# A sparse-attention and MLP kernel: first batch by casting loads, band of v gated, AV in four PSUM banks, w_out in 8 KB runs

## The chip, the cores and the metric

The kernel runs on one core of one Trainium2 chip. The core has five engines that run side by side: TensorE (PE; its weight loads are listed apart as PEld), VectorE (DVE), ScalarE (ACT), GpSimd (POOL) and SyncE (SP). Each works through its own list of instructions in order, and semaphores join the lists. Sixteen DMA engines move data between the chip's memory (HBM) and the core's SBUF. DMAs are issued by SP and ACT (the queues q1 and q10 of the profile) or by POOL (q0); only those of POOL convert float32 to float16 on the way. The metric is the time of one execution on the device in microseconds (us).

## The reference

Eight batches, eight heads, 576 positions, 64 values a head. Heads 0 to 3 attend to the last 32 positions (local heads), heads 4 to 7 to all earlier positions that agree modulo 32 (strided heads). The result is the input of a two-layer MLP.

```
mask_local   = (rel >= 0) & (rel < 32)
mask_strided = (rel >= 0) & (pos[None] % 32 == pos[:, None] % 32)
scores = np.where(masks, q @ k.T / 8, -1e9)
attn = softmax(scores);  x = (attn @ v) as 4608 tokens x 512
h = x @ w_in                    # 512 x 2048
g = s * relu(h) ** 2 + b
out = g @ w_out                 # 2048 x 512, float32
```

## The kernel before

**Tiles.** A batch's heads are worked in four pairs: 0 and 1 local, 2 and 3 strided. A pair is a chain: transpose q and k on PE (`trans`, L328), copy them out of PSUM (L271, on ACT or DVE), scores (L383), exp on ACT (L396), mask on DVE (L404), the product with v (AV, L432), whose last column is the sum of the weights, reciprocal (L446) and multiplication (L450) on DVE into `x_nat`, transpose back (L471), copy into `xT` (L271). One AV group of six or four matmuls uses one PSUM bank, and there is one such bank (tag `a`, `AB = 1`), so the next group waits for the multiplication of the group before it.

**MLP.** The tokens are cut into nine blocks of 512. FF1 (L507) is 64 matmuls a block, in groups of four over `xT[0..3]`, ReLU on ACT (L522), square on DVE (L526). FF2 (L541) is 64 matmuls a block, evicted by DVE (L552) and stored by SP. `bcs` (L564) is the constant row that b adds, 16 matmuls with w_out, needed before the first FF2 eviction.

**Loads.** For batch 0, q, k and v come as float32 by SP and ACT into staging areas (two 16 KB tiles of the pool `gT`, and `w_out_sb`, not yet in use), and are cast to float16 by ACT and DVE (`pair_post`, `cast_s`, `cast_v`). The v of the local heads is the band: for each block of 96 queries the 128 keys that it sees, 256 bytes a run, five DMAs (L210, L212). The v of batch 1 goes the same way. POOL copies one element of the staged k into `gate` (L617), which holds back everything behind it on POOL: w_in (four DMAs), q and k of batch 1, w_out (four DMAs, after the casts have read the staging area in `w_out_sb`), then q, k and v of batches 2 to 7 by casting loads.

**Order of the work.** The class `Plan` sets the order of every engine's list when the kernel is built. It keeps a clock of its own, takes costs and landing times from constants (`landing`, `plan.done`), and at each step emits a PE step that is ready by that clock; copies and casts go to ACT or DVE, whichever would be done first. The order is then fixed. If a landing comes later than assumed, the engine waits at that instruction, with all that stands behind it.

Of the kernel before, what the change touches and what calls it, by code (L numbers as in the profile page):

```python
# [106 lines left out]
def kernel(  # L107
# [31 lines left out]
    for p in range(SQ):  # L139
        for c in range(SQ):  # L140
# [39 lines left out]

    stage0 = gp.tile([128, 4096], FP32, tag="gT", name="stage0")
    stage1 = gp.tile([128, 4096], FP32, tag="gT", name="stage1")
    stage2 = w_out_sb.rearrange("p f m -> p (f m)").bitcast(FP32)
    NL, NS = 4 * LT * D, 4 * ST * D
    st_q = {"ql": stage0[0:LQ, 0:NL], "kl": stage0[0:LQ, NL:2 * NL],
            "qs": stage1[0:SQ, 0:NS], "ks": stage1[0:SQ, NS:2 * NS]}
    st_v = {0: (stage2[:, 0:NL], stage2[0:SQ, NL:NL + NS]),
            1: (stage1[:, 0:NL], stage1[0:SQ, NL:NL + NS])}

# [83 lines left out]
    def pair_post(b, name, mm, src, key, cost):  # L273

        if (b, name) not in paired:
            paired[b, name] = None

        def g(eng):
            if paired[b, name] is None:
                paired[b, name] = inp.tile([LQ, 2, LT, 2 * D], FP16, tag=name + "p",  # L280
                                           name=name + "p")
            from_ = (loaded[b, name + "l"] if src is None else src)
            copy_on(eng, out=paired[b, name][:, mm].rearrange("p j (e d) -> p e j d", e=2),
                    in_=from_.rearrange("p (m e j d) -> p m e j d", m=2, e=2, d=D)[:, mm])
        plan.post([key], cost, g, [("in", name + "l", b, mm)])

    def cast_s(name, mm, key):
        def g(eng):
            if (0, name + "s") not in loaded:
                loaded[0, name + "s"] = inp.tile([SQ, NS], FP16, tag=name + "s", name=name + "s")  # L290
            sl = slice(mm * NS // 2, (mm + 1) * NS // 2)
            copy_on(eng, out=loaded[0, name + "s"][:, sl], in_=st_q[name + "s"][:, sl])
        plan.post([key], {"A": 1030, "V": 1150}, g, [("in", name + "s", 0, mm)])

    def cast_v(b, loc, mm, key):
        nt, np_, dst = (LT, 128, v_loc) if loc else (ST, SQ, v_str)
        src = st_v[b][0 if loc else 1].rearrange("p (h t d) -> p h t d", h=4, d=D)

        def g(eng):
            hs = slice(2 * mm, 2 * mm + 2)  # L300
# [3 lines left out]
        plan.post([key], {"A": 2 * (170 + 0.83 * n), "V": 2 * (100 + 1.04 * n)}, g,  # L304
                  [("in", "vl" if loc else "vs", b, mm)])


    TB, SB, AB, F1B, F2B = 2, 2, 1, 2, 1

    def pair_steps(b, m):  # L310
# [114 lines left out]
        def av(e, j, group):  # L425
            def f():
                if j == 0 and e == 0:
                    st["x"] = xnp.tile([nq, nt, 128], FP16, tag="x" + sfx, name="x_nat")
                if j % per == 0:
                    st["a"] = psum.tile([128, 6, D + 1], FP32, tag="a", bufs=AB, name="ps_a")  # L430
                g, i = p_of(e, j)
                nc.tensor.matmul(  # L432
                    out=st["a"][0:nq, j % per, :], lhsT=st["pt", g][0:nk, i, :],
                    rhs=vt[0:nk, 2 * mm + e, j, :])

            s = Step(f, 37, needs=[("p", id_, p_of(e, j)[0]), ("in", "v" + sfx, b, mm)],
                     group=group if j % per == 0 else None)
            if j % per == per - 1:
# [61 lines left out]
    def ff1(T, ft, ct, group):  # L500
        tok0 = T * PS
        def f():
            if ft == 0 and ct == 0:
                gts[T] = gp.tile([128, NFT, PS], FP16, tag="gT", name="gT")
            if ct == 0:
                gts["h"] = psum.tile([128, PS], FP32, tag="f1", bufs=F1B, name="ps_f1")
            nc.tensor.matmul(  # L507
                out=gts["h"], lhsT=w_in_sb[:, ct, ft * 128:(ft + 1) * 128],
                rhs=xT[ct][:, tok0:tok0 + PS], start=(ct == 0), stop=(ct == 3))

        needs = [("xT", bb, ct) for bb in {tok0 // S, (tok0 + PS - 1) // S}]
        needs.append(("w_in", ft // 4))
# [89 lines left out]

    for name, at in (("q", 4600.0), ("k", 5200.0)):
        plan.done["raw", name, 0] = at
        for mm in range(2):
            pair_post(0, name, mm, st_q[name + "l"], ("raw", name, 0), {"A": 810, "V": 900})
    for name, at in (("q", 8000.0), ("k", 8600.0)):
        plan.done["raw", name + "s", 0] = at
        for mm in range(2):
            cast_s(name, mm, ("raw", name + "s", 0))  # L610
    for loc, at in ((True, 12500.0), (False, 11000.0)):
        plan.done["raw", "v", loc, 0] = at
        for mm in range(2):
            cast_v(0, loc, mm, ("raw", "v", loc, 0))

    gate = const.tile([1, 1], FP32)
    nc.gpsimd.tensor_copy(out=gate, in_=st_q["ks"][0:1, 0:1])  # L617
    load_w_in()
    ring = 13000.0
    for c in range(4):  # L620
        arrive([("w_in", c)], landing(2700))
    fetch_qk(1)

    plan.post(both("vl", 0) + both("vs", 0), {"A": 0.0}, lambda eng: load_w_out(), [("free",)])
    ring += 3000.0
    plan.done["raw", "v", True, 1] = plan.done["raw", "v", False, 1] = ring
    for c in range(4):
        arrive([("w_out", c)], landing(2700))

    def early_v():  # L630
        nc.vector.memset(
            st_v[1][0][0:LPAD].rearrange("p (h t d) -> p h t d", h=4, d=D)[:, :, 0, :], 0.0)
        stage_v(1, nc.sync, nc.sync)
        for loc in (True, False):
            for mm in range(2):
                cast_v(1, loc, mm, ("raw", "v", loc, 1))

    plan.post([("in", n, 0, mm) for n in ("qs", "ks") for mm in range(2)], {"A": 0.0},
              lambda eng: early_v(), [("early",)])

# [105 lines left out]
```

## Time and profile before

| | |
|---|---|
| runs | 372.2, 371.05, 371.8 us (median 371.8) |
| profiled execution | 374.32 us, its span 372.6 us |
| busy | PE 332.0, DVE 212.7, ACT 181.1, POOL 72.5 us |
| mean granted clock of TensorE | 0.991 |
| DMA | 66306 packets, 31.47 MB; HBM read 38.08 MB |

The span runs from the first to the last instruction; what lies around it is 374.32 - 372.6 = 1.7 us. PE's share is an average over very different stages: little is done in the first 50 us, nearly all of the time after that. Whether a change matters is seen in the stage that it touches.

### The profile page before, as it was taken

To read this page: it belongs to the slowest core of one execution; us is meant where nothing else is said; L and a number is where in the kernel's file an instruction comes from. 1 tells how busy PE (TensorE), PEld (TensorE's weight loads), DVE (VectorE), ACT (ScalarE), POOL (GpSimd) and SP (SyncE) were. 2 spreads that over 40 slices of the span, in tenths; PEclk is the share of its full clock that TensorE was granted. 3 is DMA by queue.
4 is the path that set the end of the run, shared out by engine and by line. 5 is a ranking of instruction groups with operands and counts; after the bars stand their busy time and mean duration, and the time that the engine had idled before them with its cause. 6 is when DMAs were issued, how large, how long until landed. Compare 5 with 4: busy or idle time off the path is not lost.

```text
span 372.6 us, 6416 instructions
## 1 busy us (share of the span) xinstructions
PE 332.0 (89%) x2512; PEld 186.7 (50%) x2512; DVE 212.7 (57%) x573; ACT 181.1 (49%) x332; POOL 72.5 (19%) x95
## 2 busy tenths in 40 slices
PE   1256759969999999999999999999999999899995
PEld 0244526534555555555655565555555444344442
DVE  4475748863676566666866676667566433233321
ACT  2472647853564556556554665457455243243200
POOL 0162324661062106400640260000000000000000
PEclk9999999978999999999999999999999999999999
DMA  8899999997096709911964295001100000100112
GB/s 176 185 177 194 216 216 132 129 91 81 31 132 54 99 31 129 125 34 41 129 64 83 56 120 78 2 28 42 45 30 30 28 28 32 56 29 30 56 61 80
DMA packets 66306, 31.47 MB, mean 84 GB/s; under 512 B 46244, under 2 KB 60516, under 8 KB 66276
## 3 DMA queue, kind: packets, MB, share of 16 engines
q0 software_dynamic: 52384, 16.51, 52.4%
q1 hardware_dynamic: 12748, 12.75, 11.6%
q10 hardware_dynamic: 1144, 1.80, 2.2%
q8 instruction: 19, 0.31, 0.3%
q14 instruction: 11, 0.09, 0.1%
HBM read 38.08 MB, written 9.44 MB: 128 GB/s over the span
## 4 chain that ended last, share of the span: by engine, by line
PE 77%; DMA 9%; DVE 5%; ACT 3%; SPq 3%; issue 1%; ACTq 0%; DVEq 0%
PE ps_f L507 33%; PE ps_f L541 32%; DMA w_out_sb<-in_v_dram 5%; DMA stage<-in_v_dram 4%; PE ps_a L432 3%; PE ps_t L328 3%; SPq L212 3%; PE ps_s L383 3%; PE ps_t L471 2%; DVE qD_loc L271 1%; ACT qD_loc L271 1%; DVE o L552 1%; PE ps_b L564 1%; ACT u L522 1%; DVE pt L404 1%
## 5 line engine op out<-in xcount | busy, mean ns | idle before, releaser
L507 PE MATMUL ps_f<-xT,w_in_sb 128*128 128x512 f16 x576 | 163.1, 388 | 3.3 <-ACT xT L271 3.1
L541 PE MATMUL ps_f<-w_out_sb,gT 128*128 128x512 f16 x576 | 152.6, 379 | 2.4 <-DVE o L552 2.4
L522 ACT ACTIVATE u<-ps_f 128x512 f16<-128x512 f32 x144 | 85.8, 597 | 91.0 <-PE ps_f L507 71.5
L526 DVE TENSOR_TENSOR gT<-u 128x512 f16<-128x512 f16 x144 | 59.9, 418 | 63.2 <-ACT u L522 62.0
L541 PEld LDWEIGHTS <-gT 128*128 128x128 f16 x576 | 55.7, 98 | 53.4 <-issue 3.2
L507 PEld LDWEIGHTS <-w_in_sb 128*128 128x128 f16 x576 | 56.2, 100 | 48.9 <-issue 8.1
L432 PEld LDWEIGHTS <-pt 72*72 72x72 f16 (+1 forms) x448 | 41.8, 128 | 19.9 <-DVE x_nat L450 6.8
L396 ACT ACTIVATE pt<-ps_s 128x384 f16<-128x384 f32 (+2 forms) x96 | 44.6, 490 | 13.0 <-PE ps_s L383 12.4
L450 DVE TENSOR_TENSOR x_nat<-ps_a,rec 72x256 f16<-72x256 f32 (+1 forms) x96 | 44.3, 462 | 2.0
L552 DVE SCALAR_TENSOR_TENSOR o<-ps_f,s_sb,bcs 128x512 f32<-128x512 f32 x36 | 26.9, 747 | 25.9 <-PE ps_f L541 25.2
L432 PE MATMUL ps_a<-v_str,pt 72*72 72x65 f16 x256 | 31.4, 203 | 3.7 <-DVE x_nat L450 3.6
L446 DVE RECIPROCAL rec<-ps_a 72x4 f32<-72x4 f32 (+1 forms) x96 | 17.3, 181 | 29.0 <-PE ps_a L432 28.3
L471 PE MATMUL ps_t<-ident,x_nat 72*128 72x72 f16 (+1 forms) x224 | 29.1, 210 | 2.7 <-DVE x_nat L450 2.5
L271 ACT COPY xT<-ps_t 128x576 f16<-128x576 f16 x24 | 15.3, 639 | 25.5 <-PE ps_t L471 25.5
L255 POOL DMA_DIRECT2D v_str<-in_v_dram x24 | 20.9, 870 | 30.4 <-PE ps_a L432 11.6
L383 PE MATMUL ps_s<-qD_str,kTs 128*72 128x144 f16 x128 | 26.5, 237 | 0.3 <-ACT pt L396 0.3
L471 PEld LDWEIGHTS <-x_nat 72*128 72x128 f16 (+1 forms) x224 | 17.9, 103 | 12.1 <-DVE x_nat L450 5.5
L383 PE MATMUL ps_s<-qD_loc,kT_loc 128*128 128x192 f16 x96 | 18.7, 272 | 5.9 <-ACT pt L396 4.0
L432 PE MATMUL ps_a<-v_loc,pt 128*96 128x65 f16 x192 | 22.7, 214 | 0.0
L254 POOL DMA_DIRECT2D v_loc<-in_v_dram x24 | 21.0, 876 | 7.1 <-DMA w_out_sb<-in_moe_w_out_dram 3.9
L328 PE MATMUL ps_t<-ident,qp 96*128 96x96 f16 x96 | 11.7, 224 | 10.8 <-ACT qp L271 8.0
L404 DVE TENSOR_TENSOR pt<-pt,mask_str 72x432 f16<-72x432 f16 (+1 forms) x48 | 16.4, 346 | 4.5 <-ACT pt L396 3.9
(64 smaller groups left out, 244.2 us busy)
## 6 DMA issues: line engine op xcount, KB each, us to landing
out_dram<-o SPq DMA_DIRECT2D x36, 256.0 KB, 2.0
w_in_sb<-in_moe_w_in_dram POOLq DMA_DIRECT2D x4, 512.0 KB, 11.6
w_out_sb<-in_moe_w_out_dram POOLq DMA_DIRECT2D x4, 512.0 KB, 22.6
ql<-in_q_dram POOLq DMA_DIRECT2D x7, 288.0 KB, 6.1
kl<-in_k_dram POOLq DMA_DIRECT2D x7, 288.0 KB, 6.9
qs<-in_q_dram POOLq DMA_DIRECT2D x7, 288.0 KB, 6.1
ks<-in_k_dram POOLq DMA_DIRECT2D x7, 288.0 KB, 7.7
v_loc<-in_v_dram POOLq DMA_DIRECT2D x24, 80.0 KB, 6.9
```

The costliest lines, as they stand in the source:

```text
L271: (nc.scalar.copy if eng == "A" else nc.vector.tensor_copy)(**kw)
L328: nc.tensor.matmul(out=st["p" + name][:, nq * j:nq * j + nq], lhsT=src, rhs=ident[0:nq, 0:nq], is_transpose=True)
L383: nc.tensor.matmul(out=st["s", g][0:nk, c:c + 2 * nq], lhsT=st["k"][:, i * nq:i * nq + nk], rhs=st["q"][:, i].rearrange("d e c -> d (e c)"))
L396: nc.scalar.activation(out=pt[0:nk, 0:2 * n].rearrange("k t c -> k (t c)"), in_=st["s", g][0:nk, 0:2 * n * nq], func=AF.Exp, scale=scale)
L432: nc.tensor.matmul(out=st["a"][0:nq, j % per, :], lhsT=st["pt", g][0:nk, i, :], rhs=vt[0:nk, 2 * mm + e, j, :])
L450: nc.vector.tensor_tensor(out=st["x"][:, j0:j0 + per, 64 * e:64 * e + 64], in0=st["pa", e, j][0:nq, 0:per, 0:D], in1=st["rec", e, j][0:nq, ...
L471: nc.tensor.matmul(out=st["px"][:, nq * j:nq * j + nq], lhsT=st["x"][:, j, :], rhs=ident[0:nq, 0:nq], is_transpose=True)
L507: nc.tensor.matmul(out=gts["h"], lhsT=w_in_sb[:, ct, ft * 128:(ft + 1) * 128], rhs=xT[ct][:, tok0:tok0 + PS], start=(ct == 0), stop=(ct == 3))
L522: nc.scalar.activation(out=gts["u", T, ft], in_=h, func=AF.Relu)
L526: nc.vector.tensor_tensor(out=gts[T][:, ft, :], in0=u, in1=u, op=ALU.mult)
L541: nc.tensor.matmul(out=gts["o"], lhsT=gts[T][:, ft, ts * 128:(ts + 1) * 128], rhs=w_out_sb[:, ft, :], start=(ft == 0), stop=(ft == NFT - 1))
L552: nc.vector.scalar_tensor_tensor(out=o, in0=gts["o", T, ts], scalar=s_sb[:, 0:1], in1=bcs, op0=ALU.mult, op1=ALU.add)
```

## The change

**q and k of batch 0** come by casting loads of POOL, as those of the later batches do; `cast_s` and the staging of q and k are gone. **The strided v** of batches 0 and 1 is also loaded by POOL as float16 (`vs`, one buffer) and copied into `v_str`. For these two batches each strided load is cut into partitions 0 to 63 and 64 to 71 (`load_s`). **The band of v** stays on SP in float32, but SP first issues a one-element copy out of a tile that must have landed (`after_landing`): k of the local heads for batch 0, the last quarter of w_in for batch 1. **AV of batch 0** takes its PSUM banks in turn from the tags `a`, `f1`, `f2`, `f1` (`a_group`), four banks instead of one. **w_out** is laid out so that a partition reads four neighbouring rows, one run of 8 KB in place of four of 2 KB; so that the products agree, FF1 takes every fourth column of w_in as a weight tile. **FF1** now needs all four parts of `xT` before a group begins. The constants of `Plan` that say when things land are new, and with them the order of all lists.

```diff
+    def load_s(dst, src, b):
+        for r in (slice(0, 64), slice(64, SQ)) if b < 2 else (slice(0, SQ),):
+            nc.gpsimd.dma_start(out=h4(dst)[r], in_=view_s(src, b)[r])
...
-        wv = moe_w_out.rearrange("(ft p) m -> p ft m", p=128)
+        wv = moe_w_out.rearrange("(c p l) m -> p c (l m)", p=128, l=4)
         for c in range(4):
-            nc.gpsimd.dma_start(out=w_out_sb[:, 4 * c:4 * c + 4, :], in_=wv[:, 4 * c:4 * c + 4, :])
+            nc.gpsimd.dma_start(
+                out=w_out_sb[:, 4 * c:4 * c + 4, :].rearrange("p l m -> p (l m)"), in_=wv[:, c])
...
+        tag, bufs = [("a", AB), ("f1", F1B), ("f2", F2B), ("f1", F1B)][n_a % 4 if b == 0 else 0]
...
-                out=gts["h"], lhsT=w_in_sb[:, ct, ft * 128:(ft + 1) * 128],
+                out=gts["h"], lhsT=w_in_sb[:, ct, :].rearrange("p (c x l) -> p c l x", c=4, l=4)[:, ft // 4, ft % 4],
...
-        needs = [("xT", bb, ct) for bb in {tok0 // S, (tok0 + PS - 1) // S}]
+        needs = [("xT", bb, c) for bb in {tok0 // S, (tok0 + PS - 1) // S} for c in range(4)]
...
-    nc.gpsimd.tensor_copy(out=gate, in_=st_q["ks"][0:1, 0:1])
+    def after_landing(i, src):
+        nc.sync.dma_start(out=gate[:, i:i + 1], in_=src)
+
+    fetch_qk(0)
+    early_v(0)
     load_w_in()
-    ring = 13000.0
+    after_landing(0, loaded[0, "kl"][0:1, 0:1])
+    stage_v(0)
+    plan.done["raw", "v", True, 0] = 15500.0
     fetch_qk(1)
+    after_landing(1, w_in_sb[0:1, 0, DFF - 1:DFF])
+    stage_v(1)
+    early_v(1)
+    plan.done["raw", "v", True, 1] = 40000.0
```

Where the instructions stand now (the line numbers of the changed kernel are a little lower: its copy helper is L265, exp L392, the mask L400, ReLU L520). On ACT before, around the last copy into `xT` of batch 0 (`xT_107`) and the first ReLU; `v_loc_95` and `v_str_97` are the v tiles of batch 1:

```order
L271 COPY xT_106<-ps_t 128x576
L271 COPY qD_loc_101<-ps_t 64x6x96 x2
L396 ACTIVATE pt<-ps_s 128x384 x6
L271 CAST v_loc_95<-stage_111 128x6x64 x2
L271 CAST v_str_97<-stage_111 72x8x64 x2
L271 COPY xT_107<-ps_t 128x576
L522 ACTIVATE u<-ps_f_367 128x512
```

The casts of batch 1 stand there ahead of `xT_107`. On ACT in the changed kernel, the same place; `v_loc_94` is the band tile of batch 0, `w_out_sb` its staging area:

```order
L392 ACTIVATE pt<-ps_s 72x288
L265 CAST v_loc_94<-w_out_sb 128x6x64 x4
L265 COPY xT_106<-ps_t 128x576
L265 COPY qD_str_103<-ps_t 64x8x72
L265 COPY kTs<-ps_t 128x576
L265 COPY xT_104<-ps_t 128x576
L392 ACTIVATE pt<-ps_s 72x432 x2
L392 ACTIVATE pt<-ps_s 72x288
L265 COPY xT_107<-ps_t 128x576
L520 ACTIVATE u<-ps_f_509 128x512
```

All four casts of batch 0's band are now ACT's (two were), ahead of every copy into `xT`, and no cast of batch 1 stands before `xT_107`. Those of batch 1's band have moved behind nine ReLUs, of which the last two are the first and third rows here:

```order
L520 ACTIVATE u<-ps_f_671 128x512
L392 ACTIVATE pt<-ps_s 72x288
L520 ACTIVATE u<-ps_f_684 128x512
L265 CAST v_loc_95<-stage 128x6x64 x2
L520 ACTIVATE u<-ps_f_712 128x512
```

On DVE before, the AV groups of batch 0's last strided pair: reciprocal and multiplication by turns.

```order
L446 RECIPROCAL rec<-ps_a 72x4
L450 TENSOR_TENSOR x_nat<-ps_a,rec 72x4x64
L446 RECIPROCAL rec<-ps_a 72x4
L450 TENSOR_TENSOR x_nat<-ps_a,rec 72x4x64
L271 COPY qp<-ql 96x2x6x64
L446 RECIPROCAL rec<-ps_a 72x4
```

One group is in PSUM at a time. On DVE in the changed kernel, the same pair and what follows it:

```order
L444 RECIPROCAL rec<-ps_a 72x4
L400 TENSOR_TENSOR pt<-pt,mask_str 72x288
L448 TENSOR_TENSOR x_nat<-ps_a,rec 72x4x64
L444 RECIPROCAL rec<-ps_a 72x4 x3
L448 TENSOR_TENSOR x_nat<-ps_a,rec 72x4x64 x3
L265 COPY qp<-ql 96x2x6x64 x2
L265 COPY qD_loc_100<-ps_t 64x6x96
```

Three groups now stand in PSUM together, and the copies of batch 1's q (`qp`), which stood between them, come after. On SP in the changed kernel, up to the first store:

```order
L210 DMA mask_loc<-mask_loc 128x96
L211 DMA mask_str<-mask_str 72x72
L614 DMA gate<-kl 1x1
L205 DMA w_out_sb<-in_v_dram 96x4x64
L207 DMA w_out_sb<-in_v_dram 128x5x64 x4
L622 DMA s_sb<-in_moe_s_dram 128x1
L623 DMA b_sb<-in_moe_b_dram 128x1
L614 DMA gate<-w_in_sb 1x1
L205 DMA stage<-in_v_dram 96x4x64
L207 DMA stage<-in_v_dram 128x5x64 x4
L554 DMA out_dram<-o 128x512 x36
```

Before, q, the band and the masks stood there with no wait on data in front of the band.

## Rows read from the trace of the kernel before

**Rows 1.** Busy time by stretch; columns: start:end, length, each engine (instructions), PEclk, DMA, GB/s.
```profile
0.00:38.00 38.00, 15.02 (x142) 11.95 (x142) 19.80 (x58) 16.13 (x29) 9.98 (x18) 1.00 1.02 183
38.00:51.80 13.80, 8.29 (x79) 6.30 (x80) 9.37 (x29) 8.15 (x16) 3.56 (x5) 1.00 1.21 221
51.80:70.00 18.20, 18.13 (x154) 10.32 (x154) 13.74 (x40) 12.74 (x25) 9.13 (x12) 1.00 2.35 136
70.00:90.00 20.00, 16.53 (x120) 8.57 (x118) 10.30 (x32) 11.56 (x21) 9.41 (x12) 0.83 1.72 119
90.00:350.00 260.00, 255.64 (x1940) 141.37 (x1939) 154.64 (x411) 131.88 (x243) 40.39 (x50) 1.00 0.43 58
```
**Rows 2.** The chain that ended last, in order of time: start us, us, what.
```profile
2.43 18.27 DMA w_out_sb<-in_v_dram
...
33.37 16.75 DMA stage<-in_v_dram
50.15 1.14 ACT v_str L271 x2
...
51.87 4.65 PE ps_f L507 x13
...
350.25 18.14 PE ps_f L541 x84
```
**Rows 3.** Timeline, ACT's first work on q, k and v: start us, us, instruction.
```profile
7.07 0.83 ACT L271 CAST qp<-stage 96x768 f16<-96x768 f32 x1 [2.63 <-DMA stage<-in_q_dram]
13.27 0.83 ACT L271 CAST kp<-stage 96x768 f16<-96x768 f32 x1 [5.36 <-DMA stage<-in_k_dram]
17.63 1.04 ACT L271 CAST ks<-stage 72x1024 f16<-72x1024 f32 x1
20.73 1.14 ACT L271 CAST v_str<-w_out_sb 72x512 f16<-72x512 f32 x2 [1.28 <-DMA w_out_sb<-in_v_dram]
46.54 0.92 ACT L271 CAST v_loc<-stage 128x384 f16<-128x384 f32 x2
```
**Rows 4.** Timeline, DVE at the last strided pair of batch 0.
```profile
33.47 0.18 DVE L446 RECIPROCAL rec<-ps_a 72x4 f32<-72x4 f32 x1 [0.54 <-PE ps_a L432]
33.68 0.42 DVE L450 TENSOR_TENSOR x_nat<-ps_a,rec 72x256 f16<-72x256 f32 x1
34.65 0.18 DVE L446 RECIPROCAL rec<-ps_a 72x4 f32<-72x4 f32 x1 [0.54 <-PE ps_a L432]
```
**Rows 5.** Waits from 0 to 52 us: who waited for whom, us, times, longest.
```profile
ACT qp L271 <- DMA ql<-in_q_dram: 5.5, 1, 5.5
PE ps_f L507 <- ACT xT L271: 2.9, 1, 2.9
```
**Rows 6.** POOL's issues: w_in, and the last part of w_out.
```profile
17.70 3.13 POOL L263 DMA_DIRECT2D w_in_sb<-in_moe_w_in_dram  x4
35.96 0.74 POOL L268 DMA_DIRECT2D w_out_sb<-in_moe_w_out_dram  x1 [2.69 <-DMA w_in_sb<-in_moe_w_in_dram]
```
**Rows 7.** Issue to landing of k by POOL, from 100 to 200 us.
```profile
DMA to landing us min/median/max: 5.9/6.2/6.9
```
**Rows 8.** DMA queues from 18 to 20 us: packets, MB, share of 16 engines.
```profile
q1 hardware_dynamic: 1251, 0.31, 93.1%
```
**Rows 9.** DMA queues from 28 to 42 us.
```profile
q0 software_dynamic: 2502, 2.08, 90.3%
q1 hardware_dynamic: 2500, 0.62, 32.9%
```
**Rows 10.** Issue to landing of w_out.
```profile
DMA to landing us min/median/max: 22.1/22.6/24.2
```
**Rows 11.** Weight loads by form, 60 to 350 us: line, operation, shape, count, busy us, mean ns.
```profile
L507 PEld LDWEIGHTS <-w_in_sb 128*128 128x128 f16 x549 | 53.0, 99 | 43.1 <-issue 2.9
L432 PEld LDWEIGHTS <-pt 128*96 128x96 f16 x150 | 14.7, 127 | 5.6 <-DVE x_nat L450 0.4
```
**Rows 12.** One more stretch, before the first FF2 (columns as in rows 1).
```profile
79.20:86.00 6.80, 6.28 (x38) 3.04 (x36) 2.87 (x9) 2.36 (x4) 3.91 (x5) 0.50 2.14 66
```
**Rows 13.** Page, costliest groups: exp.
```profile
L396 ACT ACTIVATE pt<-ps_s 128x384 f16<-128x384 f32 (+2 forms) x96 | 44.6, 490 | 13.0 <-PE ps_s L383 12.4
```

More of the change, by code (lines that the diff above doesn't have):

```diff
@@ L176 @@
     plan = Plan()
-    stage0 = gp.tile([128, 4096], FP32, tag="gT", name="stage0")
-    stage1 = gp.tile([128, 4096], FP32, tag="gT", name="stage1")
-    stage2 = w_out_sb.rearrange("p f m -> p (f m)").bitcast(FP32)
     NL, NS = 4 * LT * D, 4 * ST * D
[L185 to L188, printed above, removed]
+    spare = gp.tile([128, 4096], FP32, tag="gT", name="spare")
+    vl_stage = [t[:, 0:NL].rearrange("p (h t d) -> p h t d", h=4, d=D) for t in
+                (w_out_sb.rearrange("p f m -> p (f m)").bitcast(FP32),
+                 gp.tile([128, 4096], FP32, tag="gT", name="stage"))]
     def view_l(src, b):
@@ L281, in g @@
                                            name=name + "p")
-            from_ = (loaded[b, name + "l"] if src is None else src)
+            from_ = loaded[b, name + "l"]
             copy_on(eng, out=paired[b, name][:, mm].rearrange("p j (e d) -> p e j d", e=2),
                     in_=from_.rearrange("p (m e j d) -> p m e j d", m=2, e=2, d=D)[:, mm])
[L285 to L293, printed above, removed]
+        plan.post([key], {"A": 810, "V": 350}, g, [("in", name + "l", b, mm)])
     def cast_v(b, loc, mm, key):
         nt, np_, dst = (LT, 128, v_loc) if loc else (ST, SQ, v_str)
-        src = st_v[b][0 if loc else 1].rearrange("p (h t d) -> p h t d", h=4, d=D)
         def g(eng):
-            hs = slice(2 * mm, 2 * mm + 2)
+            src = vl_stage[b] if loc else loaded[b, "vs"].rearrange(
+                "p (h t d) -> p h t d", h=4, d=D)
             for h in range(2 * mm, 2 * mm + 2):
@@ L303, in cast_v, with a_group @@
         n = nt * D
[L304 removed]
+        plan.post([key], {"A": 2 * (170 + 0.83 * n),
+                          "V": 2 * (100 + 1.04 * n) if loc else 2 * (100 + 0.55 * n)}, g,
                   [("in", "vl" if loc else "vs", b, mm)])
     TB, SB, AB, F1B, F2B = 2, 2, 1, 2, 1
+    n_a = 0
+    def a_group(b):
+        nonlocal n_a
+        tag, bufs = [("a", AB), ("f1", F1B), ("f2", F2B), ("f1", F1B)][n_a % 4 if b == 0 else 0]
+        n_a += 1
+        return Group(tag, bufs)
     def pair_steps(b, m):
@@ L601, in fetch_v @@
         arrive(both("vl", b) + both("vs", b), landing(7000))
[L603 to L614, printed above, removed]
@@ L616, with early_v @@
-    gate = const.tile([1, 1], FP32)
-    nc.gpsimd.tensor_copy(out=gate, in_=st_q["ks"][0:1, 0:1])
-    load_w_in()
-    ring = 13000.0
+    def early_v(b):
+        loaded[b, "vs"] = inp.tile([SQ, NS], FP16, tag="vs", bufs=1, name="vs")
+        load_s(loaded[b, "vs"], v, b)
+        plan.done["raw", "v", False, b] = landing(2100)
+        for loc in (True, False):
+            for mm in range(2):
+                cast_v(b, loc, mm, ("raw", "v", loc, b))
+    gate = const.tile([1, 4], FP16)
+    def after_landing(i, src):
+        nc.sync.dma_start(out=gate[:, i:i + 1], in_=src)
@@ L620 @@
+    ring = 2500.0
+    fetch_qk(0)
+    early_v(0)
+    load_w_in()
+    after_landing(0, loaded[0, "kl"][0:1, 0:1])
+    stage_v(0)
+    nc.sync.dma_start(out=s_sb, in_=moe_s.to_broadcast([128, 1]))
+    nc.sync.dma_start(out=b_sb, in_=moe_b.to_broadcast([128, 1]))
+    plan.done["raw", "v", True, 0] = 15500.0
     for c in range(4):
-        arrive([("w_in", c)], landing(2700))
+        arrive([("w_in", c)], landing(3200))
     fetch_qk(1)
-    plan.post(both("vl", 0) + both("vs", 0), {"A": 0.0}, lambda eng: load_w_out(), [("free",)])
@@ L625 @@
-    ring += 3000.0
-    plan.done["raw", "v", True, 1] = plan.done["raw", "v", False, 1] = ring
+    after_landing(1, w_in_sb[0:1, 0, DFF - 1:DFF])
+    stage_v(1)
+    early_v(1)
+    plan.done["raw", "v", True, 1] = 40000.0
+    plan.post(both("vl", 0), {"A": 0.0}, lambda eng: load_w_out(), [("free",)])
+    ring += 1500.0
     for c in range(4):
         arrive([("w_out", c)], landing(2700))
[L630 to L636, printed above, removed]
```

39 lines of the change are left out of this document (15 added, 24 removed).

## The prediction

> **What bounds the kernel now.** I read the table by stretch first, then the chain of waits in order of time, then the timeline of the start, the DMA queues, and last the instruction lists of both programs. The table shows two kernels in one. From 90 to 350 us PE is busy 255.64 of 260 us [rows 1]: there the time is PE's work and nothing in the change makes it less. From 0 to 51.8 us PE is busy 15.02 + 8.29 = 23.3 us [rows 1]; 28.5 us go by without work. The chain says on what: the band of v for batch 0 lands at 2.43 + 18.27 = 20.7 us, the v of batch 1 at 33.37 + 16.75 = 50.1 us, ACT casts it, and FF1 starts in earnest at 51.87 us [rows 2]. In between lies batch 0's attention, 31 us from the first cast of v (20.73) to FF1 [rows 2, 3], which is a chain of short steps: one AV group every 34.65 - 33.47 = 1.18 us [rows 4], with DVE and ACT also stuck on batch 1's q (5.5 us on ACT) and at the end FF1 waiting 2.9 us for a copy that stands behind batch 1's v on ACT [rows 5]. A second, smaller loss lies between 70 and 90 us: PE idle 3.5 us, granted clock 0.83 [rows 1], and 0.50, the 1.2 GHz level, from 79.2 to 86 us [rows 12], after PE had run out of ready FF work.
>
> So the change is worth what it does to the time at which FF1 starts, less what it then makes FF1 wait for.
>
> **k and q.** Before, q lands at 7.07 and k at 13.27 us, the strided k is cast at 17.63 us [rows 3]. In the changed kernel POOL issues `kl` as its third DMA, at about 2 us; such a load lands 6.2 us after its issue when little else runs [rows 7], so k is there at 8.2 us, 5 us earlier, and q a little before it, not earlier than now. Four float32 casts of the strided q and k go, the other casts become copies of float16; they lie beside waits for DMA, and as time on the path I count them at nothing. This gain is not the end of the chain, since v ends it.
>
> **The band of v, batch 0.** It is now issued behind the landing of k, at 8.3 us, with five issues and no wait between them, about 1.1 us to the first packet. It has 384 + 4 x 640 = 2944 packets of 256 bytes. Alone they go at 1251 in 2 us [rows 8], 4.7 us for all. But then q0 is full: the strided q, k, v and 2048 packets of w_in are queued behind k. Where q0 and the band ran side by side before, from 28 to 42 us, each got 2500 packets in 14 us, 179 per us [rows 9]; at that rate the band takes 16.5 us. With some 1.5 us from the last packet to the landing it is there at 8.3 + 1.1 + 16.5 + 1.5 = 27.5 us, later than the 20.7 us of before; alone, at 15.5 us. I take the loaded rate, because the same two kinds of packets are queued. w_in, 2048 packets at the same rate behind the rest of batch 0, is complete at about 26 us, not a wait (before it was 10 us later).
>
> **From the band to FF1.** What can be done without the band is done by then: scores and exps of three pairs, and AV of the first strided pair, whose v comes by POOL. After the last band the rest stands on ACT in this order: the last cast 0.46 us [rows 3], four copies of about 0.64, three exps of 0.49 [rows 13], then mask and AV 0.8, four reciprocals of 0.18 and four multiplications of 0.42 [rows 4] in one run because the four groups have banks of their own, the transposes 0.45 and the last copy 0.64: 0.46 + 2.56 + 1.47 + 0.8 + 2.4 + 1.1 = 8.8 us, and 1.2 us for the hand-overs between engines. FF1 starts at 27.5 + 10 = 37.5 us instead of 51.87: **-14.4 us**. The band alone at 15.5 us would still leave the chain of q, k and the three other pairs, some 27 us; bounds 27 and 42 us.
>
> **What the earlier start does not bring.** Before, PE did batch 1's first pairs while it waited, part of the 8.29 us of 38 to 51.8 us [rows 1], at the slow pace of that stretch (the first FF1 matmuls take 4.65 / 13 = 358 ns, late ones 18.14 / 84 = 216 [rows 2]). At full pace and without batch 0's share this is 4 us of work that now comes after FF1's start: **+4 us** (3 to 5).
>
> **The wait that is added.** The band of batch 1 waits for the last of w_in, 26 us; at the rate of rows 9 it would land at 26 + 1.1 + 16.5 + 1.5 = 45 us. Behind w_in, though, q0 holds batch 1 and then w_out, whose 512 packets are four times as long as now. Packets took turns one for one in rows 9; if that holds, the band gets 512 turns, not 2048, in the 10 us or so of w_out, and lands at about 54 us (45 to 62). ACT meets its two casts of that band behind nine ReLUs, that is after 36 FF1 matmuls (36 x 216 ns, 1.9 us more for a slow start) and about 3 us of batch 1's attention: 37.5 + 12.7 = 50.2 us. Behind them on ACT wait all further ReLUs, hence the FF1 banks; PE can fill two more groups, 8 x 0.216 = 1.7 us. So 54 - 50.2 - 1.7 gives **+2.5 us** with the gap's after-effects (0 to 10). On POOL the first part of w_out waits for the casts of batch 0's band, 28 us, with the loads of batch 2 behind it; before, the last part was issued at 35.96 us, held by a landing of w_in [rows 6], and landed 24 us later [rows 10], so nothing is lost: w_out is there at about 46, not 60 us.
>
> **The stretch from 70 to 90 us.** With w_out earlier, the planner puts bcs and two FF2 groups before the second FF1 block, so PE has dense work while batch 1's last pairs finish. What it can give back is 3.5 us idle and half of 6.8 us [rows 1, 12]; the order there is all new, so I take **-1.5 us** (-6 to +2).
>
> **The strided weight tiles.** FF1's 576 weight loads now pick every fourth column. A load takes 99 ns, the slowest form 127 ns [rows 11], both under the 216 ns of the matmul beside which they run. I take 0. No load of this trace is strided: bounds 0 and, if each cost 28 ns more with none of it hidden, 16 us. TensorE: Matmul & The Clock Gate of the Trainium skill (Weight-path perf modes) says that the fast weight load reads four chunks of 32 columns, packed or strided, with a column step of up to 1,024; no run here shows it, and by it the term would be 0 too.
>
> **Sum.** -14.4 + 4 + 2.5 - 1.5 = -9.4 us. The profiled execution goes from 374.3 (span 372.6 and 1.7 around it) to 364.9; it lay 2.5 us above the median of the runs, so against 371.8 I forecast **362.4 us**.
>
> **Rivals.**
> (a) *The bands end last, more than I count* (slower). Place: ACT's casts of batch 1's band, with all ReLUs behind them. For: two gates one behind the other, small packets against long ones, and SP's two broadcasts of one number to 128 partitions stand between. Each us past 52 costs one. The gain is gone when the band lands at 63.5 us, and if it moves only after w_out (46 + 16.5 + 1.5 = 64 us) and PE's clock falls in the gap as it did at 79.2 us (3.4 us [rows 12]), the time is 371.8 - 14.4 + 4 + 12 + 3.4 - 1.5 = 375 us. Against: in rows 9 the small packets got their turns.
> (b) *The bands come sooner.* If a queue's turn is worth more than one small packet, batch 0's band nears its pace alone, lands at 20 us, FF1 starts at 31, batch 1's band costs nothing: -20.9 + 4 + 0 - 1.5 = -18.4, with the PE work of batch 1 then waiting for its q and k (+2): 355.5 us. DMA: Bandwidth & Descriptors of the Trainium skill (Queues, rings and completion order) has an engine change queues only after a packet of some 9 to 17 descriptors, by which several of the band's runs would go in one turn. Rows 9 speak against it, one for one.
> (c) *The strided loads are not hidden.* If a load took 392 ns, four times 99, each FF1 matmul would take 176 ns longer: 576 x 0.176 = 101 us, 463 us. Nothing in the profile speaks for it but that no such load is there.
> (d) *The start does not move the end*: batch 0 sooner, but FF1 starves on batch 1 and w_out as now, since the DMA engines carry the same data: about 371 us. For: DMA share is 1.0 or more from 0 to 52 us [rows 1]. Against: FF1 of the first block needs only batch 0 and w_in.
>
> **How the numbers follow.** My forecast 0.58 (357.5 to 367.5 us by its own terms), (a) 0.15, (b) 0.17, (c) 0.03, (d) 0.07. The range 355.5 to 371.5 us takes in (b), (d) and the milder half of (a). A measurement here tells about 0.3%, 1.1 us, from no change. Faster by more: forecast, (b), and a third of (a), 0.80; within: most of (d) and a little of (a), 0.08; slower: the rest of (a) and (c), 0.12.
>
> **What would show it.** In the changed profile: `kp` copied near 8.5 us; ACT's last cast of `v_loc` from `w_out_sb` near 28 us; the last `xT` copy of batch 0 and FF1 near 37.5 us; a wait of ACT on `stage<-in_v_dram` near 50 us, some 4 us long; FF1's weight loads still near 99 ns; no stretch at 0.50 near 80 us; 90 to 350 us as full as now. I am wrong if FF1 starts after 45 us, if ACT's wait on batch 1's band passes 10 us, or if FF1 matmuls in a dense row are farther apart than 216 ns.

## The result and the profile after

The changed kernel takes **362.96 us** (median of 4 runs, 362.03 to 363.34), the kernel before 371.54 us (371.05 to 372.2) on the same chip: ratio 0.9764, 95% interval 0.9738 to 0.9791. The forecast was 362.4 us. The profiled execution is 362.61 us long, its span 360.8 us.

The table by stretch, answering to [rows 1] with the same columns; the last line is the stretch of [rows 12]:

```profile
0.00:38.00 38.00, 13.95 (x144) 12.13 (x144) 17.16 (x55) 12.90 (x24) 18.41 (x33) 1.00 1.12 179
38.00:51.80 13.80, 12.18 (x101) 7.36 (x101) 9.29 (x30) 8.39 (x17) 4.85 (x7) 1.00 1.14 202
51.80:70.00 18.20, 17.32 (x153) 10.45 (x152) 14.27 (x44) 14.31 (x29) 9.42 (x12) 1.00 2.01 130
70.00:90.00 20.00, 19.32 (x199) 12.10 (x196) 14.24 (x43) 13.28 (x25) 6.65 (x9) 1.00 0.83 89
90.00:350.00 260.00, 255.76 (x1894) 144.00 (x1893) 150.53 (x399) 131.26 (x240) 39.15 (x49) 1.00 0.39 58
...
79.20:86.00 6.80, 6.80 (x79) 4.56 (x78) 5.62 (x18) 5.14 (x10) 2.08 (x3) 1.00 0.91 124
```

PE's busy time up to 38 us has fallen by 1 us; from 38 to 51.8 us it rose from 8.29 to 12.18 us, from 70 to 90 us from 16.53 to 19.32, there at the full clock (mean 0.83 before); from 51.8 to 70 us it fell by 0.8 us, and from 90 to 350 us PE is as full as before. The chain in order of time, answering to [rows 2], says what the start now hangs on:

```profile
2.63 5.47 DMA kl<-in_k_dram
8.12 0.73 SPq L614
...
14.41 18.72 DMA w_out_sb<-in_v_dram
33.16 0.52 ACT v_loc L265
...
41.67 2.56 PE ps_f L505 x6
...
53.89 0.86 PE ps_f L505 x4
```

It is the band of v, now behind the landing of k (8.12 us, the gate is L614), and it is there at 33.16 us. Before, DVE began to cast it at 22.22 us:

```profile
22.22 0.62 DVE L271 CAST v_loc<-w_out_sb 128x384 f16<-128x384 f32 x2
```

(What lands at 20.7 us in [rows 2] is the strided v, which ACT issued and which was cast into `v_str`; the prediction calls it the band.) So the band comes 11 us later than before, but from the last band to FF1 it takes 8.5 us, where it took nearly 30. The v of batch 1 no longer stands in the chain. The timeline of ACT (start, length, instruction, idle time before it and what ended it), answering to [rows 3]:

```profile
8.76 0.83 ACT L265 COPY kp<-kl 96x768 f16<-96x768 f16 x1
...
20.68 0.51 ACT L265 CAST v_loc<-w_out_sb 128x384 f16<-128x384 f32 x1 [2.73 <-DMA w_out_sb<-in_v_dram]
...
33.16 0.51 ACT L265 CAST v_loc<-w_out_sb 128x384 f16<-128x384 f32 x1 [4.07 <-DMA w_out_sb<-in_v_dram]
...
41.70 0.64 ACT L265 COPY xT<-ps_t 128x576 f16<-128x576 f16 x1 [3.00 <-PE ps_t L469]
...
55.70 0.92 ACT L265 CAST v_loc<-stage 128x384 f16<-128x384 f32 x2
```

ACT waits four times for band 0 (up to 4.07 us) and not at all for band 1: the last line has no bracket. It was close: the last part of band 1 landed at 55.74 us, and ACT's second cast, which reads it, began at 56.1. Why band 0 is late is seen at SP (issues: start, time that the issuing took) and in the queues (packets, MB, share of 16 engines), first from 9 to 12 us, then from 14 to 32 us, which answer to [rows 9]:

```profile
8.12 0.73 SPq L614 DMA_DIRECT2D gate<-kl  x1
8.89 0.80 SPq L205 DMA_DIRECT2D w_out_sb<-in_v_dram  x1
9.74 8.69 SPq L207 DMA_DIRECT2D w_out_sb<-in_v_dram  x4
...
26.81 18.58 SPq L207 DMA_DIRECT2D stage<-in_v_dram  x4
```
```profile
q0 software_dynamic: 646, 0.56, 121.9%
```
```profile
q0 software_dynamic: 3051, 2.76, 92.1%
q1 hardware_dynamic: 3049, 0.72, 31.5%
```

From 9 to 12 us no packet of SP's queue q1 moves although the gate was issued at 8.12. The gate's own two bytes pass at 12.26 us, the first packet of the band at 12.95. After that the queues go one for one, 3049 packets in 18 us, 169 per us, and SP stands in its issues (8.69 and 18.58 us for four).

The weight loads on the page of the profile (count, busy us, mean ns), answering to [rows 11]: FF1's strided tiles, then FF2's contiguous ones.

```profile
L505 PEld LDWEIGHTS <-w_in_sb 128*128 128x128 f16 x576 | 63.8, 114 | 42.9 <-issue 1.6
...
L539 PEld LDWEIGHTS <-gT 128*128 128x128 f16 x576 | 55.4, 98 | 53.3 <-issue 5.5
```

### The profile page after: what moved, and what is told of

It reads as the page before. It is cut to its first block, busy times and chain, and to the rows that moved or that the text cites. A ratio compares the mean times of both kernels' runs of the same rounds, so it can differ in the third digit from the quotient of the medians.

```text
span 360.8 us, 6423 instructions
## 1 busy us (share of the span) xinstructions
PE 325.3 (90%) x2512; PEld 188.9 (52%) x2512; DVE 207.7 (58%) x569; ACT 180.1 (50%) x332; POOL 78.5 (22%) x107
## 4 chain that ended last, share of the span: by engine, by line
PE 83%; DMA 7%; DVE 4%; ACT 2%; SPq 2%; issue 1%; POOL 0%; DVEq 0%; ACTq 0%; POOLq 0%
PE ps_f L505 35%; PE ps_f L539 33%; DMA w_out_sb<-in_v_dram 5%; PE ps_a L430 4%; PE ps_s L379 4%; PE ps_t L324 4%; PE ps_t L469 2%; DVE o L550 2%; DMA kl<-in_k_dram 2%; SPq L207 1%; DVE qD_loc L265 1%; PE ps_b L562 1%; ACT qD_loc L265 1%; ACT u L520 1%; DVE x_nat L448 0%
## 5 line engine op out<-in xcount | busy, mean ns | idle before, releaser
L505 PE MATMUL ps_f<-xT,w_in_sb 128*128 128x512 f16 x576 | 157.0, 383 | 0.0
L520 ACT ACTIVATE u<-ps_f 128x512 f16<-128x512 f32 x144 | 85.7, 597 | 76.4 <-PE ps_f L505 67.4
L505 PEld LDWEIGHTS <-w_in_sb 128*128 128x128 f16 x576 | 63.8, 114 | 42.9 <-issue 1.6
L430 PEld LDWEIGHTS <-pt 72*72 72x72 f16 (+1 forms) x448 | 40.3, 126 | 28.2 <-issue 12.1
L392 ACT ACTIVATE pt<-ps_s 128x384 f16<-128x384 f32 (+2 forms) x96 | 44.6, 492 | 12.7 <-PE ps_s L379 12.1
L430 PE MATMUL ps_a<-v_str,pt 72*72 72x65 f16 x256 | 30.2, 203 | 0.6 <-DVE pt L400 0.4
L265 ACT COPY xT<-ps_t 128x576 f16<-128x576 f16 x21 | 13.4, 638 | 31.5 <-PE ps_t L469 31.5
L469 PE MATMUL ps_t<-ident,x_nat 72*128 72x72 f16 (+1 forms) x224 | 27.2, 209 | 0.9 <-DVE x_nat L448 0.9
L379 PE MATMUL ps_s<-qD_str,kTs 128*72 128x144 f16 x128 | 24.6, 238 | 1.6 <-ACT kTs L265 0.8
L400 DVE TENSOR_TENSOR pt<-pt,mask_str 72x432 f16<-72x432 f16 (+1 forms) x48 | 16.6, 350 | 6.0 <-ACT pt L392 5.0
L239 POOL DMA_DIRECT2D qs<-in_q_dram x10 | 6.8, 680 | 60.3 <-PE ps_t L324 53.8
L379 PE MATMUL ps_s<-qD_loc,kT_loc 128*128 128x192 f16 x96 | 17.3, 259 | 2.0 <-ACT pt L392 1.0
## 6 DMA issues: line engine op xcount, KB each, us to landing
w_in_sb<-in_moe_w_in_dram POOLq DMA_DIRECT2D x4, 512.0 KB, 11.7
```

The costliest lines, as they stand in the source:

```text
L379: nc.tensor.matmul(out=st["s", g][0:nk, c:c + 2 * nq], lhsT=st["k"][:, i * nq:i * nq + nk], rhs=st["q"][:, i].rearrange("d e c -> d (e c)"))
L392: nc.scalar.activation(out=pt[0:nk, 0:2 * n].rearrange("k t c -> k (t c)"), in_=st["s", g][0:nk, 0:2 * n * nq], func=AF.Exp, scale=scale)
L430: nc.tensor.matmul(out=st["a"][0:nq, j % per, :], lhsT=st["pt", g][0:nk, i, :], rhs=vt[0:nk, 2 * mm + e, j, :])
L469: nc.tensor.matmul(out=st["px"][:, nq * j:nq * j + nq], lhsT=st["x"][:, j, :], rhs=ident[0:nq, 0:nq], is_transpose=True)
L505: nc.tensor.matmul(out=gts["h"], lhsT=w_in_sb[:, ct, :].rearrange("p (c x l) -> p c l x", c=4, l=4)[:, ft // 4, ft % 4], rhs=xT[ct][:, tok ...
L520: nc.scalar.activation(out=gts["u", T, ft], in_=h, func=AF.Relu)
```

## Experiments

All times are medians of 4 runs (e1: of 10); the ratio is to the kernel before on the same chip. FF1 start and PE's busy time up to 90 us are from each profile; before had 51.9 and 57.98 us.

| run | FF1 start | PE busy 0 to 90 | us | ratio (95%) |
|---|---|---|---|---|
| changed kernel | 41.5 | 62.76 | 362.96 | 0.9764 (0.9738 to 0.9791) |
| e1 one bank | 54.2 | 55.69 | 372.02 | 1.0017 (0.9998 to 1.0035) |
| e2 w_out in 2 KB runs | 40.8 | 63.80 | 361.84 | 0.9747 (0.9725 to 0.9769) |
| e3 no first gate | 29.6 | 64.96 | 363.77 | 0.9793 (0.9769 to 0.9817) |
| e4 before + four banks | 40.8 | 64.72 | 358.66 | 0.9662 (0.9638 to 0.9687) |
| e5 no first gate, band 1 early | 30.4 | 73.16 | 351.17 | 0.9455 (0.9439 to 0.9471) |
| e6 before + needs line | 47.7 | 63.69 | 363.78 | 0.9794 (0.9775 to 0.9814) |
| e7 bands by POOL | 29.9 | 73.50 | 350.75 | 0.9443 (0.9424 to 0.9462) |
| e8 first gate, band 1 early | 41.3 | 61.16 | 363.09 | 0.9776 (0.9746 to 0.9805) |
| e9 e7 with 2 KB runs | 29.9 | 73.68 | 350.69 | 0.9448 (0.9423 to 0.9474) |
| e10 e3 with 2 KB runs | 30.1 | 69.33 | 358.16 | 0.9625 (0.9603 to 0.9647) |

The third column, PE's work up to 90 us, goes with the time better than the second does (work done slowly, at half clock, counts in it too): e3 starts FF1 12 us before the changed kernel and ends no sooner. What the two share is the landing of the last part of batch 1's band, read from the traces: 55.7 us in the changed kernel and 55.5 in e3. It is 58.6 us in e8, 51.9 in e2, 50.8 in e10, and only 37.5 in e5 and 37.8 in e7, which are among the fastest.

**e1: the changed kernel with one AV bank.**
```diff
-        tag, bufs = [("a", AB), ("f1", F1B), ("f2", F2B), ("f1", F1B)][n_a % 4 if b == 0 else 0]
+        tag, bufs = [("a", AB), ("f1", F1B), ("f2", F2B), ("f1", F1B)][0]
```


> The changed kernel with one PSUM bank for the AV groups of batch 0 again (all else kept; the planner orders anew). My theory (the time follows the start of FF1, and that follows the band's landing plus the chain behind it): the last cast of the band stays near 33 us, the groups behind it take turns at 1.2 us each, FF1 starts 3 to 5 us later than the 41.5 us of the changed kernel, and the time is 365 to 368 us instead of 363. Rival (the banks don't matter since the strided pair's AV fits in the wait for the band): FF1 at 41 to 42.5 us, 362 to 364 us.

372.02 us: the whole gain is gone, more than expected. The waits from 0 to 60 us (us in total, times, longest):

```profile
PE ps_a L430 <- DVE x_nat L448: 17.7, 5, 14.2
...
DVE v_loc L265 <- DMA w_out_sb<-in_v_dram: 13.3, 2, 9.9
```
and the last band on the chain:
```profile
32.20 0.36 DVE v_loc L265
```

DVE, which here had casts of the band on its list, stood on the landing; the multiplication that frees the only bank stood behind it, and PE at the next AV group for 14.2 us. From the last band (32.20 us) it still took 22 us to FF1 instead of 8.5. Four banks, with the lists that go with them, are worth 372.02 - 362.96 = 9.1 us in this kernel; that two of the band's casts went to DVE is a part of those lists, and its share was not measured by itself.

**e2: the changed kernel with w_out and FF1's weights as before.**
```diff
-        wv = moe_w_out.rearrange("(c p l) m -> p c (l m)", p=128, l=4)
+        wv = moe_w_out.rearrange("(ft p) m -> p ft m", p=128)
```
(with the two places that use the layout)

> The changed kernel with the w_out layout of before (2 KB runs) and so contiguous weight tiles for FF1. My theory: neither the landing of w_out nor the weight loads are waited for; w_out then takes 2048 turns against the band of batch 1, lands later (52 to 56 us instead of 48) while the band lands sooner (about 50 us); FF1's weight loads are at 99 ns again instead of 114; FF1 starts at 41.5 us as now; 362 to 364 us. Rival (the 8 KB runs are a part of the gain): the first matmul with w_out waits, 365 us or more. Second rival (the strided loads cost time in the changed kernel): 15 ns x 576 = 8.6 us at most come back, 355 to 361 us.

361.84 us, 1.1 us under the changed kernel, with intervals that overlap: the 8 KB runs and the strided loads together bring nothing and cost at most about that. The two were not taken apart, but the strided loads, 63.8 us in all, are hidden: four FF1 matmuls in a row take 0.86 us in the changed kernel (the chain at 53.89 us), 215 ns each.

**e3: the changed kernel without the gate before band 0.**
```diff
-    after_landing(0, loaded[0, "kl"][0:1, 0:1])
```


> The changed kernel without the gate in front of the band of batch 0: SP issues it right after the masks. My theory: the band, the last to land in the changed kernel, lands earlier (20 to 26 us instead of 33), k later (11 to 14 us instead of 8.5); the chain behind still needs the strided pairs, FF1 starts at 33 to 38 us; 355 to 360 us. Rival (the gate earns the gain by letting q and k land alone): k, scores and exps come late, FF1 starts at 42 us or later, 363 us or more.

The casts of band 0 start at 18.41 us and FF1 at 29.63, sooner than my theory had it, and the time is 363.77, as in the rival. ACT's timeline shows where the 12 us went:

```profile
52.52 0.52 ACT L265 CAST v_loc<-stage 128x384 f16<-128x384 f32 x1 [8.54 <-DMA stage<-in_v_dram]
55.52 0.51 ACT L265 CAST v_loc<-stage 128x384 f16<-128x384 f32 x1 [2.48 <-DMA stage<-in_v_dram]
```

ACT reaches band 1 at 44 us and waits 11.0 us there, with all ReLUs behind it. PE is busy 8.91 of 13.8 us from 38 to 51.8 us and 12.81 of 18.2 us after that, at a mean clock of 0.87 and 0.72. That is rival (a) of the prediction, which the changed kernel escapes only because band 0 makes it late enough, by 0.4 us: the band of batch 1 lands at the same time in both.

**e4: the kernel before with four AV banks** (and FF1's needs line, without which an FF1 group that has begun holds a bank which AV needs to bring it its last input).
```diff
+        tag, bufs = [("a", AB), ("f1", F1B), ("f2", F2B), ("f1", F1B)][n_a % 4 if b == 0 else 0]
...
-        needs = [("xT", bb, ct) for bb in {tok0 // S, (tok0 + PS - 1) // S}]
+        needs = [("xT", bb, c) for bb in {tok0 // S, (tok0 + PS - 1) // S} for c in range(4)]
```


> The kernel before with one part of the change alone: four PSUM banks for the AV groups of batch 0 (and FF1 groups that wait for all four parts of xT, as the banks of FF1 are now shared). My theory: in the kernel before the chain of AV groups is about 27 us long but mixed with waits for batch 1's q and v; FF1 can't start before the casts of batch 1's v on ACT (landing at 50.1 us), so FF1 starts at 50 to 52 us as before and the time is 369 to 372 us. Rival (the AV chain was what held the start): FF1 at 40 to 45 us, 362 to 367 us.

358.66 us, against my expectation: these two edits alone give more than the whole change. DVE's timeline at the last strided pair, answering to [rows 4], and what DVE and PE do next:

```profile
31.39 0.18 DVE L455 RECIPROCAL rec<-ps_a 72x4 f32<-72x4 f32 x1
31.49 0.39 DVE L459 TENSOR_TENSOR x_nat<-ps_a,rec 72x256 f16<-72x256 f32 x1
31.86 0.18 DVE L455 RECIPROCAL rec<-ps_a 72x4 f32<-72x4 f32 x1
```
```profile
36.02 0.36 DVE L271 COPY qp<-ql 96x768 f16<-96x768 f16 x1 [3.67 <-DMA ql<-in_q_dram]
36.30 0.41 DVE L459 TENSOR_TENSOR x_nat<-ps_a,rec 72x256 f16<-72x256 f32 x1
...
39.51 0.76 DVE L271 COPY xT<-ps_t 128x576 f16<-128x576 f16 x1
```
```profile
36.91 0.66 PE L335 MATMUL ps_t<-ident,qp 96*128 96x96 f16 x6 [4.08 <-ACT qp L271]
...
40.76 1.48 PE L516 MATMUL ps_f<-xT,w_in_sb 128*128 128x512 f16 x3
```

An AV group takes 31.86 - 31.39 = 0.47 us, not 1.18. Three of the four parts of `xT` are there at 32.3 us. The last multiplication stands on DVE's list behind a copy of batch 1's q, which comes at 36 us, and batch 1's transposes stand before the last ones of batch 0 on PE's; so the fourth part of `xT` is there at 40.3 us and FF1 starts at 40.76.

**e5: the changed kernel without the first gate, band 1 behind k of batch 0.**
```diff
-    after_landing(0, loaded[0, "kl"][0:1, 0:1])
...
-    after_landing(1, w_in_sb[0:1, 0, DFF - 1:DFF])
+    after_landing(1, loaded[0, "kl"][0:1, 0:1])
```


> The changed kernel without the gate before batch 0's band, and with the band of batch 1 gated on k of batch 0 instead of the last quarter of w_in, so that it is loaded some 15 us sooner. Theory A (the start of FF1 is worth its time one for one as soon as no later landing takes its place; taking only the first gate away gave nothing because ACT then stood 11.0 us on batch 1's band): FF1 starts at 30 to 34 us, ACT waits under 3 us for stage, no half clock between 38 and 70 us, and the time is 352 to 357 us. Theory B (before 52 us the work of batch 1 and the loads of q, k and w_out set the pace whichever band lands when): FF1 starts as early, but the time stays at 360 to 364 us and some other wait of about 10 us shows on PE or ACT before 60 us.

351.17 us, theory A, a little under its range. The first stretches, and ACT at band 1, without a wait:

```profile
0.00:38.00 38.00, 22.72 (x222) 17.25 (x223) 23.65 (x76) 18.57 (x35) 16.25 (x30) 1.00 1.14 180
38.00:51.80 13.80, 13.80 (x119) 8.50 (x118) 11.55 (x37) 11.10 (x24) 7.45 (x9) 1.00 1.13 207
```
```profile
44.38 0.92 ACT L265 CAST v_loc<-stage 128x384 f16<-128x384 f32 x2
```

**e6: the kernel before with the needs line alone** (the second part of e4's diff).

> The kernel before, with only the one line by which an FF1 group waits for all four parts of xT; one AV bank as before. It is the half of the earlier run with four banks that is not the banks. Theory A (the banks gave the whole 12.8 us): 370.5 to 372.5 us, FF1 in earnest at 51 to 53 us, PE's AV still waiting some 12 us or more for the multiplications of x_nat. Theory B (the order of the lists, changed by that line, gave part of it): 360 to 368 us.

363.78 us, theory B: this line moves the lists enough for 7.4 us (371.14 to 363.78). FF1 starts 4.2 us sooner and there is no stretch at half clock before 90 us. About 2 us of the 4.2 are not the line's. ACT's list is the same in both kernels up to the band's casts, yet it cast k here at 11.43 us, against 13.27 in [rows 3]:

```profile
11.43 0.83 ACT L271 CAST kp<-stage 96x768 f16<-96x768 f32 x1 [4.50 <-DMA stage<-in_k_dram]
```

So the profiled execution of before was late from its loads on, by 1.8 us; that may be most of the 2.5 us by which it lay above its median. The banks' own part in e4, again with the lists that go with them, is 363.78 - 358.66 = 5.1 us.

**e7: the changed kernel with both bands as casting loads of POOL** into `v_loc`: no staging, gates or casts of the band, w_out not held.
```diff
-        nc.sync.dma_start(out=vl_stage[b][LPAD:128, :, 0, :], in_=first)
+        nc.gpsimd.dma_start(out=v_loc[b][LPAD:128, :, 0, 0:D], in_=first)
...
-    fetch_qk(0)
+    fetch_qk(0, lambda: stage_v(0))
```


> The changed kernel with the bands of batches 0 and 1 as casting loads of POOL straight into v_loc, as the later batches have them: batch 0's behind the local k, batch 1's behind its q and k; no staging, no gates, no casts of the band on ACT, w_out issued without waiting. Theory A (one queue in the order of need beats two that share the engines): the band of batch 0 lands at 13 to 18 us, w_in is whole by 30 us, FF1 starts at 30 to 36 us, the time is 351 to 357 us. Theory B (ten more issues on POOL at 0.9 us each and 5888 small packets ahead of w_in and w_out push these back by what the band gains): FF1 waits for w_in or starts at 38 to 44 us and the time is 359 to 366 us.

350.75 us, theory A at the edge of its range, 12.2 us under the changed kernel and as good as e5. POOL issues the four large parts of the band from 4.13 to 7.56 us:

```profile
4.13 3.43 POOL L203 DMA_DIRECT2D v_loc<-in_v_dram  x4
```

The band lands at 13.5 us. PE begins its product with the local v at 17.25 us and FF1 at 29.94. This edit changes the queue, the gates, the casts and the release of w_out at once; as e5, with the band on SP, is as fast, the run doesn't show that one queue is better than two.

**e8: the changed kernel with band 1 behind k of batch 0** (the second part of e5's diff alone).

> The changed kernel with its first gate, and the band of batch 1 gated on k of batch 0 (so issued right behind batch 0's band) instead of the last quarter of w_in. It completes the square with the runs without the first gate. Theory A (two waits one behind the other on the way to FF1's first groups; taking away the one that does not end last is worth nothing): FF1 starts at 40 to 43 us as in the changed kernel, where ACT came to batch 1's band only after it had landed, and the time is 361 to 365 us. Theory B (the early load of batch 1's band is what gave the 12 us, for instance by clearing the queues for w_out): 351 to 356 us.

363.09 us, in the range of theory A, but not by its way: the edit did not bring band 1 forward. SP's issues, and ACT at band 1:

```profile
23.61 0.84 SPq L614 DMA_DIRECT2D gate<-kl  x1
24.49 0.38 SPq L205 DMA_DIRECT2D stage<-in_v_dram  x1
24.92 20.30 SPq L207 DMA_DIRECT2D stage<-in_v_dram  x4
```
```profile
58.59 0.52 ACT L265 CAST v_loc<-stage 128x384 f16<-128x384 f32 x1 [2.30 <-DMA stage<-in_v_dram]
```

SP gets to that gate only at 23.61 us, behind its issues of band 0 and of two small loads; in the changed kernel the second gate is issued at 25.72 us. The last part of the band lands at 58.6 us, 2.8 us later than there, and ACT waits 2.3 us for it. So e8 does not test an early band 1 behind a late band 0. The nearest run to that is e2, where band 1 lands at 51.9 us, 3.8 us before the changed kernel's, and the time is 1.1 us lower. What the runs show: the first gate taken away by itself gives nothing (e3); with the second moved to k as well, which then does bring band 1 forward, 11.8 us (e5).

**e9: e7 with w_out and FF1's weights as before** (e2's diff).

> The version with both bands as casting loads of POOL, with w_out in 2 KB runs and FF1's weight tiles contiguous, as before the change. Theory A (the strided weight loads, 114 ns against 99, cost about 1 us through the places where a load is not covered, and the 8 KB runs give nothing back): 349 to 350.3 us, 0.4 to 1.5 us under that version's 350.75. Theory B (there w_out is nearer to being late, bcs came 3.6 us after ACT was free, and four times as many packets put it back): 351.5 to 354 us.

350.69 us, the same as e7: inconclusive between the theories, and the layout is worth nothing there either way.

**e10: e3 with w_out and FF1's weights as before.**

> The changed kernel without the first gate (363.8 us, where ACT stood 11.0 us on batch 1's band), and besides with w_out in 2 KB runs and FF1's weight tiles contiguous, as before the change; the second gate stays on the last quarter of w_in. Theory A (the queues take turns packet by packet, so the band of batch 1 gets 512 turns while the 8 KB runs pass, in packets of 4096 bytes, and four times as many while 2 KB runs pass): the band lands some 8 to 10 us sooner, ACT waits under 3 us for stage, and the time is 351 to 356 us. Theory B (the second gate alone makes that band late, whatever it shares the engines with): ACT still waits 8 us or more and the time is 361 to 364 us, as the run with 8 KB runs.

358.16 us: theory A in its mechanism, half of it in size, and outside both ranges. The queues from 34 to 44 us, of e3 and of this run:

```profile
q0 software_dynamic: 553, 1.99, 98.5%
q1 hardware_dynamic: 443, 0.11, 8.0%
```
```profile
q0 software_dynamic: 1563, 1.55, 91.3%
q1 hardware_dynamic: 1566, 0.39, 30.0%
```
and ACT's wait for batch 1's band here (us, times, longest), 11.0 us in e3:
```profile
ACT v_loc L264 <- DMA stage<-in_v_dram: 5.8, 2, 3.0
```

While the 8 KB runs pass (481 of q0's 553 packets write 4096 bytes), band 1 gets 443 turns in 10 us; beside 2 KB runs it gets 1566, and its last part lands at 50.8 us instead of 55.5. So the 8 KB runs do cost something as soon as a small-packet load that is waited for lies beside them: 363.77 - 358.16 = 5.6 us here.

## Why the prediction was right, and where its terms were not

- **k and q.** k was forecast to land at 8.2 us and did at 8.1. Right.
- **Band 0.** Forecast 27.5 us, found 33.2: the term "8.3 + 1.1 + 16.5 + 1.5" (27.4, as written) was too small. From the gate's issue (8.12) to the band's first packet (12.95) lie 4.8 us and not 1.1 (q1 stands still from 9 to 12 us). The 2944 packets take 19.4 us, to 32.3, and not 16.5: the loaded rate is 169 per us, not 179, and some 280 packets of 4 bytes, which the forecast did not count, pass among them. From the last packet to the landing it is 0.8 us; the 1.5 us of the forecast stood in no row. The choice of the loaded rate over the pace alone was right. That the Trainium skill's rule (DMA: Bandwidth & Descriptors, Queues, rings and completion order), a turn of 9 to 17 descriptors, would favour the band is not borne out: 3051 packets to 3049, and in e10 1563 to 1566, where the start times also alternate, one of each queue about every 100 ns on an engine.
- **From the band to FF1.** Forecast 10 us, found 8.5 (33.16 to 41.67). Right, and e1, where it takes 22 us with one bank, says that the four banks and their lists make it so. With the needs line (7.4 us in e6) the banks carry the gain; the prediction hid both inside the -14.4 us and gave neither a price of its own.
- **FF1's start.** Forecast 37.5, found 41.5 us: -10.4 instead of -14.4 between the profiles, roughly the band's 5.7 us less the 1.5 us above.
- **The wait on band 1.** Forecast: landing at 54 us, ACT there at 50.2, +2.5 us. The band landed at 55.7, 1.7 us after the forecast, and ACT's casts at 55.7 and 56.1 just missed waiting for it: 0. That w_out's long packets hold such a band is seen in e10. ACT came late because FF1 did: the first miss removed this term, by luck. In e3, where FF1 starts early, the wait is 11.0 us.
- **The stretch from 70 to 90 us.** Forecast -1.5 us (-6 to +2). PE gave back 2.8 us of idle time there (16.53 to 19.32 us busy), and the half clock of [rows 12] is gone. What is left of the profiled difference, -11.7 + 10.4 - 4 = -5.3 us, I put to this stretch, near the end of its range; the 4 us in it were not measured by themselves. Read from the stretch itself it comes to about the same: 2.8 us of idle time and, at half clock, half of the 6.28 us busy in [rows 12], 3.1 us, together 5.9. So the mechanism was right and the size was not. The half clock is no matter of the profile alone: the mean granted clock on record for each run of before is 0.986 to 0.991 (0.991 in the profile), for each run of the changed kernel 0.998 to 1.000.
- **Strided weight loads.** Forecast 0 and 99 ns. Each takes 114 ns, still hidden under the matmuls (215 ns from one to the next); e2 and e9 bound the layout with its loads at 1.1 us. (Rival (c) takes 392 ns as four times 99, which is 396.) The Trainium skill (TensorE: Matmul & The Clock Gate, Weight-path perf modes) lets the fast weight load read packed or strided columns and names no price for the stride; the trace shows 15 ns a load.
- **Rivals.** (a) is real, as e3 shows, but the changed kernel does not reach its point; (b) and (c) did not happen. The outcome of (d), that the start does not move the end, came in e3, but by the wait of (a).

So the time came out within 0.6 us of the forecast, partly by misses that cancel: FF1 4 us later, no ACT stall (2.5), more given back after 70 us (3.8), and the 2.5 us by which the profile of before lay above its median, which the profile after does not (362.61 to 362.96). And the larger fact was not forecast: the rest of the change, without its banks and the needs line, loses. At one bank it costs 372.02 - 363.78 = 8.2 us against e6, at four 362.96 - 358.66 = 4.3 us against e4. The late bands do it: e5, the same change with both bands brought forward, is 358.66 - 351.17 = 7.5 us under e4.

## What to carry to other kernels

When a change has several parts, give each a price of its own: here the banks and the needs line carry 12.8 us (e4), and the rest costs a third of it. Before a wait on the path is shortened, look which landing the same engine waits for next: in e3 the second wait took the whole gain of the first, and it came only when both were shortened (e5). A moved gate is not yet a moved landing: read the landing in the trace (e8). A load that is needed first should be issued first; here it made no difference whether it then went in one queue in the order of need (e7) or beside it in a second (e5). Long runs should not lie beside small-packet loads that are waited for (e3, e10).

## What the runs showed of the hardware

- Two DMA queues shared the engines about one packet for one even when most of q0's packets were 4096 bytes long (553 to 443 in e3), so the queue with 256-byte packets fell to 8.0% of the engines.
- SP was held in its issues when much was queued ahead: 20.30 us for four issues in e8, where the first four of e3 took 2.72 us. A gate or another load behind them comes that much later.
- After standing still, q1 took 4.1 us from the gate's issue to its 2 bytes while q0 was busy (8.12 to 12.26 us here, 27.12 to 31.25 us in e3); the first load of the kernel took 1.0 us to its first packet (0.73 to 1.70 us). Why is not settled.
- A 128x128 float16 weight tile of every fourth column loads in 114 ns against 98 to 99 contiguous.
